# Squares of late chunks on ScalarE alone, statistics of token rows on GpSimd, and another order table

## The chip, the core and the metric

The kernel runs on one core of a Trainium2 chip. The metric is the time of the device for one execution, in microseconds (us); lower is better. The core has five engines that run side by side, each through its own list of instructions in the order of that list: TensorE (PE, matrix products into PSUM), VectorE (DVE), ScalarE (ACT), GpSimd (POOL) and SyncE (SP, which only issues DMAs). An instruction that waits holds up everything behind it on its engine.

## What is computed

Attention without softmax, normalised by token and head, and then a feed-forward layer on the 4608 tokens:

```python
kv = np.einsum('bhsd,bhse->bhde', k, v)          # 8 batches, 8 heads, 576 tokens, 64
out = np.einsum('bhsd,bhde->bhse', q, kv)
rms = np.sqrt(np.mean(out * out, axis=-1, keepdims=True) + 1e-06)
x = (out / rms * g_norm)                         # rows of 512 = 8 heads x 64
h = x @ w_in                                     # 512 -> 1024
solu = h * softmax(h)
ln = (solu - mu) / np.sqrt(var + 1e-06) * g_ln   # over the 1024
y = ln @ w_out                                   # 1024 -> 512
```

The softmax's denominator and the mean need not be applied to the elements. With e = exp(h) and u = h * e, the output rows are u @ (w_out scaled by g_ln and centred), times one factor for each token, and this factor follows from three sums over the 1024 features of a token: z = sum(e), usum = sum(u) and qsum = sum(u * u). "Statistics" below means the combination qsum - usum^2 / 1024 + 1e-6 * 1024 * z^2 (up to a common factor), whose reciprocal square root is the factor.

## The kernel before, in words

The 4608 tokens are nine chunks of 512. Chunks 0 to 7 hold the first 512 tokens (in the order of the load) of one batch each, chunk 8 the 64 that are left of every batch. The work is cut into some 700 named pieces. Each piece is a Python function that issues a few instructions; `plan.add` (in class `Plan`, line 34) gives it a name, the engine or engines on which it may run, the pieces that must stand ahead of it, and the buffers that it takes. The string `ORDER` (line 68) lists all pieces once, and the kernel issues them in that order. So the table fixes, for each engine, the order of its instructions, and with `@` and `/` also the buffer and the engine: `b3.1/act@ob6` is piece b3.1 on ScalarE into buffer ob6. Between engines nothing is ordered but by semaphores: a piece waits for what it reads and for the buffer that it takes over. A piece that stands early in the table on an idle engine runs early, whatever stands around it.

Buffers are slots (line 19): PSUM banks P0 to P2 (two banks each) and S0, S1; in SBUF L0 to L7 and M0 to M12 (large), osq, lss, rst, and ob0 to ob6 for output rows.

The pieces that the prediction speaks of, for chunk c, group m of 128 tokens, and half or part p:

- `k`, `v`, `q` (L269): load of a batch, 576 KB written as bf16 from f32, issued from GpSimd's queue (batches 0 and 1 in two halves `a`, `b` of 288 KB). `wi`, `wo` load the weights. The n-th DMA of that queue also waits until the one eight before it has landed.
- `kv` (L314) and its copies out of PSUM `kc` (L173 on ScalarE, L175 on VectorE): the 64x64 products of all heads of a batch.
- `qt`/`qc` (L359): q turned by TensorE for chunks 0 to 4. For chunks 5 to 8 `qx` (L370) turns it by a DMA transpose that SyncE issues.
- `o` (L407; L470 for chunks 6 to 8): out = q @ kv. For chunks 0 to 5 the squares `sq` (L420), their means by TensorE `s` (L435), `ln` (L439) and `ex` (L443) give the norm, and `x` (L453) applies it. For chunks 6 to 8 the tokens lie on the partitions: `sq` (L479), `vd` (L483), `vl` (L489, L491), `vg` on GpSimd (L495), `x` (L504), and `xt` (L512), a DMA transpose.
- `h`, the product with w_in: chunks 0 to 2 with features on the partitions (L572), chunks 3 to 8 with tokens (L581), two halves of four matmuls for each m, such as h4.00 and h4.01.
- `e` = exp(h) on ScalarE (L592; for token rows L599, which also sums z) and `u` on VectorE (L607; for token rows L612, with usum).
- `r`, the squares of u. For chunks 0 to 2 they are elements (L622 on ScalarE, L624 on GpSimd), summed later by TensorE with z and usum in `z` (L691), after `g` (L643) on GpSimd has added up e. For token rows `r` sums as it squares: L630 on ScalarE or L632 on VectorE, as the table says.
- `t` (L637): the rows of u turned by a DMA transpose from SyncE, chunks 3 to 8.
- `gate` (L343): a copy of one element on GpSimd that reads the last load, q of batch 7. The transposes t of all chunks from 3 on wait for it, and each qx waits for t3.0. So no DMA transpose is in flight beside the loads.
- `st`: the statistics (L703 to L708 for chunks 0 to 2; four small VectorE instructions, L714 to L720, for chunks 3 to 8), `rs` their reciprocal square root on ScalarE (L726, L728).
- `a` (L767; L774 for the last two quarters): product with w_out, two halves for each m. `b` (L782 on ScalarE, L784 on VectorE) multiplies by the factor into an ob buffer, and `d` (L799 for chunks 6 to 8, two DMAs each; L801) stores it, from the queue of SyncE, GpSimd or (chunk 8) ScalarE. `ql` copies the last rows of each q for chunk 8, `warm` are matmuls on zeros, `gb` loads g_norm for L495.

## Time and profile before

| | us |
|---|---|
| median of 3 runs | 182.08 (182.04 to 183.93) |
| the profiled execution, its own time | 181.77 |
| its span, first to last instruction | 179.7 |
| mean granted clock of TensorE | 0.999 of full speed |
| last matmul ends at | 174.86 |
| last load of q (batch 7): issued, landed | 70.94, 88.70 |

A page of the profile describes one execution. Times in it are from the start of the span. A group row gives the line, the engine, the operation, output and input, the count, then busy time and the mean ns of one, then the idle time of the engine just before these instructions and what ended it. A row of waits gives who waited for whom, and total, times, longest. A row of the DMA view gives the size of one DMA and the time from issue to landing. A timeline row gives start, length, engine, line and count; the engines' queues that only issue are written SPq, ACTq. In the chain of work that ended last, each piece is what released the next.

### The profile page before, as it was taken

The page shows a single profiled execution, that of the slowest core. Times are in us where ns is not written, and L with a number is a line of the kernel's source. Part 1 is how long each engine was busy: PE and PEld are TensorE (multiplying, and loading weights), DVE is VectorE, ACT ScalarE, POOL GpSimd, SP SyncE. Part 2 cuts the span into 40 slices and gives each one's busy share as a digit, 9 for nine tenths or more (in the row PEclk, how much of TensorE's full clock was granted, in tenths as well). Part 3 has the DMA queues.
Part 4 walks back from the last instruction along what each step waited for, and adds up shares of the span by engine and source line. Part 5 has one row for each costly group of instructions (what it writes and reads, how often), then busy time and mean ns, then how long its engine had stood idle before and what let it go on. Part 6 is the DMA issues. An engine that isn't in the chain of part 4 may idle for free.

```text
span 179.7 us, 4520 instructions
## 1 busy us (share of the span) xinstructions
PE 164.9 (92%) x1808; PEld 81.1 (45%) x1831; DVE 127.1 (71%) x222; ACT 128.1 (71%) x239; POOL 71.9 (40%) x83
## 2 busy tenths in 40 slices
...
DMA  5999999999999999999799999999998689968994
GB/s 170 252 207 275 353 208 209 205 208 222 248 233 232 209 207 198 277 214 206 157 172 203 206 216 220 152 256 245 171 227 239 99 166 248 200 139 215 175 256 125
DMA packets 60424, 37.81 MB, mean 210 GB/s; under 512 B 42140, under 2 KB 55204, under 8 KB 60404
## 3 DMA queue, kind: packets, MB, share of 16 engines
...
## 4 chain that ended last, share of the span: by engine, by line
PE 63%; DMA 22%; DVE 6%; issue 3%; POOL 1%; SPq 1%; ACT 1%; POOLq 0%; DVEq 0%; ACTq 0%
PE ps_S L767 20%; PE ps_P L581 19%; DMA sb_M<-in_q_dram 9%; PE ps_P L572 8%; PE ps_P L767 5%; DMA out_dram<-sb_ob 4%; DMA sb_L<-in_v_dram 4%; DMA sb_M<-sb_M 3%; PE ps_S L359 2%; DVE sb_ob L784 2%; PE ps_P L314 2%; PE ps_P L407 2%; DMA sb_L<-sb_L 2%; PE ps_P L691 1%; PE ps_S L435 1%
## 5 line engine op out<-in xcount | busy, mean ns | idle before, releaser
L767 PE MATMUL ps_S<-w_out_sb,sb_L 128*128 128x512 bf16 x220 | 53.1, 379 | 2.9 <-issue 2.4
L581 PE MATMUL ps_P<-w_in_sb,sb_M 128*128 128x512 bf16 x188 | 42.7, 379 | 1.0 <-ACT kvd L173 0.8
L767 PEld LDWEIGHTS <-sb_L 128*128 128x128 bf16 x280 | 26.4, 98 | 33.4 <-issue 3.3
L612 DVE SCALAR_TENSOR_TENSOR sb_L<-ps_P,sb_M 128x1024 bf16<-128x1024 f32 x24 | 29.1, 1222 | 8.4 <-ACT sb_M L599 8.2
L599 ACT ACTIVATE sb_M<-ps_P 128x1024 f32<-128x1024 f32 x24 | 24.5, 1023 | 8.2 <-PE ps_P L581 7.1
L581 PEld LDWEIGHTS <-sb_M 128*128 128x128 bf16 x192 | 18.7, 98 | 23.3 <-issue 0.9
L495 POOL TENSOR_TENSOR sb_M<-rr,g_rep 128x1024 f32<-128x1024 f32 x6 | 12.3, 2061 | 30.4 <-ACT rr L491 23.7
L572 PE MATMUL ps_P<-sb_M,w_in_sb 128*128 128x512 bf16 x94 | 21.9, 379 | 0.1
L607 DVE TENSOR_TENSOR sb_L<-ps_P,sb_M 128x1024 bf16<-128x1024 f32 x12 | 14.6, 1222 | 8.2 <-ACT sb_M L592 8.2
L453 DVE SCALAR_TENSOR_TENSOR sb_M<-ps_P,g_cols,sb_rst 128x512 bf16<-128x512 f32 x24 | 18.0, 790 | 2.9 <-ACT sb_rst L443 2.6
L784 DVE TENSOR_SCALAR sb_ob<-ps_S,rstd 128x512 f32<-128x512 f32 (+1 forms) x19 | 13.8, 735 | 7.7 <-PE ps_S L767 2.2
L592 ACT ACTIVATE sb_M<-ps_P 128x1024 f32<-128x1024 f32 x12 | 12.2, 1024 | 6.9 <-PE ps_P L572 6.9
L643 POOL TENSOR_TENSOR sb_M<-sb_M 128x512 bf16<-128x512 f32 x12 | 15.1, 1278 | 4.9 <-ACT sb_M L592 4.8
L420 ACT ACTIVATE sb_osq<-ps_P 128x512 bf16<-128x512 f32 x24 | 13.4, 596 | 4.6 <-PE ps_P L407 4.6
L630 ACT ACTIVATE sb_M<-sb_L 128x1024 bf16<-128x1024 bf16 x14 | 14.6, 1047 | 0.0
L572 PEld LDWEIGHTS <-w_in_sb 128*128 128x128 bf16 x96 | 9.2, 98 | 10.5 <-issue 0.2
L801 POOL DMA_DIRECT2D out_dram<-sb_ob x10 | 6.3, 633 | 16.4 <-DVE sb_ob L784 8.8
L632 DVE SCALAR_TENSOR_TENSOR sb_M<-sb_L 128x1024 bf16<-128x1024 bf16 x10 | 12.8, 1276 | 0.1
L443 ACT ACTIVATE sb_rst<-sb_lss 128x512 f32<-128x512 f32 x20 | 12.0, 632 | 0.1
L767 PE MATMUL ps_P<-w_out_sb,sb_L 128*128 128x512 bf16 x47 | 11.4, 379 | 0.1
L206 PE MATMUL ps_S<-zeros 128*128 128x512 bf16 (+1 forms) x18 | 8.5, 591 | 1.8 <-DVE zeros L188 1.5
L624 POOL TENSOR_TENSOR sb_L<-sb_L 128x1024 bf16<-128x1024 bf16 x4 | 7.6, 1910 | 6.1 <-DVE sb_L L607 6.0
...
## 6 DMA issues: line engine op xcount, KB each, us to landing
...
sb_L<-in_k_dram POOLq DMA_DIRECT2D x6, 576.0 KB, 12.2
sb_L<-in_v_dram POOLq DMA_DIRECT2D x6, 576.0 KB, 13.1
sb_M<-in_q_dram POOLq DMA_DIRECT2D x6, 576.0 KB, 12.3
...
sb_M<-in_q_dram POOLq DMA_DIRECT2D x4, 288.0 KB, 7.0
```

The lines of the kernel that those rows point to most:

```text
L420: nc.scalar.activation(out=t[:, :], in_=T["o", c, hf][:, z], func=AF.Square)
L453: nc.vector.scalar_tensor_tensor(out=T["x", c][:, pairs_of(c, hf), :, z], in0=T["o", c, hf][:, z].rearrange("p (n q) -> p n q", n=2), scal ...
L572: nc.tensor.matmul(t[:, f % 2], w_in_sb[:, dt, f * 128:(f + 1) * 128], T["x", c][:, dt].rearrange("p q z -> p (q z)"), start=(dt == 0), st ...
L581: nc.tensor.matmul(T["h", c, m][:, half], x_block(c, m, dt), w_in_sb[:, dt, half * 512:half * 512 + 512], start=(dt == 0), stop=(dt == NP ...
L599: nc.scalar.activation(out=t.rearrange("p a b -> p (a b)"), in_=T["h", c, m].rearrange("p a b -> p (a b)"), func=AF.Exp, accum_out=T["zsum ...
L607: nc.vector.tensor_tensor(out=flat(T["u", c][:, 2 * p:2 * p + 2, :]), in0=flat(T["h", c, p]), in1=flat(T["e", c, p]), op=MUL)
L612: nc.vector.scalar_tensor_tensor(out=T["un", c][:, m, :], in0=T["h", c, m].rearrange("p a b -> p (a b)"), scalar=1.0, in1=T["e", c, m].rea ...
L630: nc.scalar.activation(out=unused, in_=src, func=AF.Square, accum_out=by)
L632: nc.vector.scalar_tensor_tensor(out=unused, in0=src, scalar=1.0, in1=src, op0=MUL, op1=MUL, accum_out=by)
L643: nc.gpsimd.tensor_tensor(out=T["es", c][:, n, :], in0=e[:, 0, :], in1=e[:, 1, :], op=ADD)
L767: nc.tensor.matmul(T["acc", c, m][:, 0], T["u", c][:, f, m * 128:(m + 1) * 128], w_out_sb[:, f, :], start=(f == 0), stop=(f == NF - 1))
L784: nc.vector.tensor_scalar_mul(out=t[:, :], in0=src, scalar1=T["rstd", c][:, m:m + 1])
```

## The change

Three things change. First, the squares `r` of chunks 4 to 8 may only run on ScalarE; those of chunk 3 may still run on either, and all four are on VectorE in the new table. Second, the statistics of chunks 3 to 8 become six element-wise products and sums on GpSimd, with two constant tiles that VectorE fills once at the start. Third, the whole order table is another one. The change in the code:

```diff
@@ -197,6 +197,10 @@
     factors = big.tile([128, 4, 2], FP32, name="factors")
     nc.vector.memset(factors[:, :, 0:1], -1.0)
     nc.vector.memset(factors[:, :, 1:2], 1e-6 * d_ff * d_ff)
+    per_u = big.tile([128, 4], FP32, name="per_u")
+    nc.vector.memset(per_u, -1.0 / d_ff)
+    per_z = big.tile([128, 4], FP32, name="per_z")
+    nc.vector.memset(per_z, 1e-6 * d_ff)
 
 
     def warm(i):
@@ -675,7 +679,7 @@
                          [("M", ("e", c, m))], [("h", c, m)])
                 plan.add(f"u{c}.{m}", "dve", lambda c=c, m=m: row_u(c, m), [f"e{c}.{m}"] + [f"u{c}.0"] * (m > 0),
                          [] if m else [("L", ("un", c))], [("h", c, m), ("e", c, m)] + [("un", c)] * (m > 0))
-                plan.add(f"r{c}.{m}", ("act", "dve"), lambda e, c=c, m=m: row_usq(c, m, e), [f"u{c}.{m}"],
+                plan.add(f"r{c}.{m}", ("act", "dve") if c < 4 else ("act", "act"), lambda e, c=c, m=m: row_usq(c, m, e), [f"u{c}.{m}"],
                          uses=[("un", c), ("e", c, m)])
                 plan.add(f"t{c}.{m}", "sp", lambda c=c, m=m: u_turn(c, m), [f"u{c}.{m}"] + [f"t{c}.0"] * (m > 0) + ["gate"] * (c >= GATED),
                          [] if m or c == GATED else [("L", ("u", c))], [("un", c)] + [("u", c)] * (m > 0 or c == GATED))
@@ -707,19 +711,19 @@
         T["vare", c] = small.tile([128, 4], FP32, name="vare")
         nc.vector.tensor_reduce(out=T["vare", c][:, :], in_=terms[:, :, :], op=ADD, axis=mybir.AxisListType.X)
 
-    def row_stats(c, ms=slice(0, 4)):
-        zs, us, qs = (T[name, c][:, ms] for name in ("zsum", "usum", "qsum"))
-        n = ms.stop - ms.start
-        a = small.tile([128, n], FP32, name="a")
-        nc.vector.scalar_tensor_tensor(out=a[:, :], in0=us, scalar=-1.0 / d_ff, in1=us, op0=MUL, op1=MUL)
-        d = small.tile([128, n], FP32, name="d")
-        nc.vector.scalar_tensor_tensor(out=d[:, :], in0=zs, scalar=1e-6 * d_ff, in1=zs, op0=MUL, op1=MUL)
-        f = small.tile([128, n], FP32, name="f")
-        nc.vector.tensor_tensor(out=f[:, :], in0=a[:, :], in1=qs, op=ADD)
-        T["vare", c] = small.tile([128, n], FP32, name="vare")
-        nc.vector.scalar_tensor_tensor(
-            out=T["vare", c][:, :], in0=f[:, :], scalar=1.0, in1=d[:, :], op0=MUL, op1=ADD
-        )
+    def row_stats(c):
+
+        def product(name, in0, in1, op):
+            t = small.tile([128, 4], FP32, name=name)
+            nc.gpsimd.tensor_tensor(out=t[:, :], in0=in0[:, :], in1=in1[:, :], op=op)
+            return t
+
+        a = product("a", T["usum", c], T["usum", c], MUL)
+        a = product("a2", a, per_u, MUL)
+        f = product("f", a, T["qsum", c], ADD)
+        d = product("d", T["zsum", c], T["zsum", c], MUL)
+        d = product("d2", d, per_z, MUL)
+        T["vare", c] = product("vare", f, d, ADD)
 
     def rstd(c):
         lv = small.tile([128, 4], FP32, name="lv")
@@ -735,7 +739,7 @@
             plan.add(f"y{c}", "dve", lambda c=c: sums_turn(c), [f"z{c}"], uses=[("sum", c)])
             plan.add(f"st{c}", "dve", lambda c=c: stats(c), [f"y{c}"], uses=[("sum", c)])
         else:
-            plan.add(f"st{c}", "dve", lambda c=c: row_stats(c), [f"{n}{c}.{m}" for n in "eur" for m in range(4)])
+            plan.add(f"st{c}", "pool", lambda c=c: row_stats(c), [f"{n}{c}.{m}" for n in "eur" for m in range(4)])
         plan.add(f"rs{c}", "act", lambda c=c: rstd(c), [f"st{c}"])
```

The table, where the prediction follows it (in the new kernel all line numbers of the functions are higher by 4):

```diff
 ORDER = """
-warm0@S0 k0a@L0,L1 v0a rsqrt q0a@M0 k0b ident qt0.0@S0 cast0.0/act cast0.1/dve kv0a@P0 kc0a.1/act v0b q0b wi0
-kc0a.2/act gr warm1@S1 tg@S1 qc0.0/dve@M1 kc0a.0/act o0.0@P0 sq0.00@osq0 sq0.01@osq1 warm2@S0 kv0b@P1 kc0b.0/act
-kc0b.1/dve s0.00@S0 ex0.00@rst0 kc0b.2/act qt0.1@P2 qc0.1/dve s0.01@S0 ex0.01@rst1 warm3@P1 o0.1@P2 sq0.10@osq1
-sq0.11@osq0 warm4@S0 s0.10@S0 warm5@P1 gm@M2 x0.00@M1 ex0.10@rst0 s0.11@S1 x0.01 x0.10 ex0.11@rst1 x0.11 wi1
-h0.0+@P0 wo0@L2 h0.1+ h0.2+@P1 h0.3+ h0.0 h0.1 h0.2 wo1@L3 table e0.0@M3 u0.0@L1 h0.4+@P2 k1a@L0 h0.5+ v1a h0.3 h0.4
-e0.1@M4 h0.5 e0.2@M5 h0.6+@P0 h0.7+ q1a@M6 k1b v1b g0.0@M7 g0.1 g0.2 r0.0/act@L4 h0.6 h0.7 e0.3@M1 g0.3 wm0@S1 u0.1
-r0.1/act u0.2 u0.3 r0.2/act r0.3/act wm1 wc4 kv1a@P2 kc1a.1/act kc1a.0/act warm6@S0 qt1.0@S0 z0@P0 warm7@P1
-kc1a.2/act wc1 wc2 qc1.0/act@M1 o1.0@P2 warm8@S0 wc3 sq1.00@osq0 sq1.01@osq1 kv1b@P1 kc1b.1/act kc1b.2/act wc5 wc0
...
-s2.10@S1 s2.11@P1 ln2.10@lss1 g1.0@M8 g1.1 g1.2 b0.3/dve@ob0 ln2.11@lss0 a1.00@S0 ex2.10@rst2 ex2.11@rst3 x2.00@M3
-q4@M0 k5@L1 v5 x2.01 x2.10 r1.1/pool r1.2/pool r1.3/act ql3/act a1.01 kv3@P2 kc3.1/act qt3.0@S1 x2.11 h2.0@P0 h2.1
-h2.2@P1 h2.3 kc3.0/act qc3.0/act@M4 d0.2/sp d0.3/sp kc3.2/act h2.4@P2 h2.5 g1.3 q5@M5 qt3.1@S1 e2.0@M9 g2.0@M7
-e2.1@M10 e2.2@M11 u2.0@L4 u2.1 h2.6@P0 h2.7 e2.3@M3 g2.1 g2.2 qc3.1/dve u2.2 k6@L2 qt4.0@S1 o3.0@P1 sq3.00@osq0
-qc4.0/dve@M10 r2.0/act@L6 r2.1/pool u2.3 r2.2/act z1@P2 y1 st1 rs1 b1.0/dve@ob0 d1.0/sp a1.10@S1 a1.11 a1.20@P0
-r2.3/act s3.00@P2 ln3.00@lss0 a1.21 b1.1/dve@ob2 b1.2/dve@ob1 g2.3 z2@S0 sq3.01@osq0 y2 ex3.00@rst3 st2 o3.1@P2
-sq3.10@osq1 s3.01@S1 ln3.01@lss0 a1.30@P0 sq3.11@osq0 ex3.01@rst2 s3.10@S0 ln3.10@lss1 ex3.10@rst0 x3.00@M4 x3.01
-a1.31 a2.00@S1 s3.11@S0 ln3.11@lss0 kv4@P1 ex3.11@rst2 kc4.0/act a2.01 v6 q6@M3 k7@L0 rs2 b1.3/dve@ob3 v7 q7@M7
-d1.1/sp d1.2/sp x3.10 kv5@P0 kc4.2/dve kc5.1/act kc4.1/dve o4.0@P1 sq4.00@osq0 x3.11 ql5/pool qt4.1@S0 qc4.1/act
-sq4.01@osq1 kc5.0/dve kc5.2/dve h3.00@P2 h3.01 h3.10@P0 e3.0@M8 b2.0/dve@ob1 s4.00@S0 ln4.00@lss0 s4.01@S1
-ln4.01@lss1 h3.11 e3.1@M11 ex4.00@rst2 a2.10@S0 a2.11 u3.0@L1 u3.1 ex4.01@rst0 x4.00@M1 x4.01 o4.1@P2 a2.20@S1
-b2.1/act@ob2 a2.21 d1.3/pool gate@L3 t3.0 t3.1 qx5@M10 sq4.10@osq1 s4.10@S0 sq4.11@osq0 s4.11@P0 b2.2/dve@ob0
-ln4.10@lss1 ln4.11@lss0 r3.0/dve ex4.10@rst0 ex4.11@rst2 x4.10 h3.20@P1 h3.21 h3.30@P0 qx6@M8 x4.11 h3.31 h4.00@P2
-h4.01 e3.2@M9 u3.2 e3.3@M4 e4.0@M12 r3.1/act r3.2/dve a2.30@S0 u3.3 t3.2 t3.3 d2.0/sp h4.10@P1 u4.0@L5 h4.11
-r3.3/dve e4.1@M11 u4.1 gb r4.0/act h4.20@P0 h4.21 h4.30@P2 st3 e4.2@M4 u4.2 h4.31 e4.3@M1 o5.0@P1 sq5.00@osq0
-sq5.01@osq1 rs3 a2.31 a3.00@S1 s5.00@P0 ln5.00@lss0 b2.3/dve@ob3 u4.3 a3.01 b3.0/dve@ob4 ex5.00@rst2 x5.00@M12
-s5.01@S0 ln5.01@lss1 kv6@P0 kc6.1/dve kc6.2/dve t4.0@L4 d2.1/sp t4.1 t4.2 kc6.0/dve o5.1@P2 sq5.10@osq1 ex5.01@rst0
-sq5.11@osq0 d2.2/pool x5.01 a3.10@S1 s5.10@S0 ln5.10@lss1 ql7/pool a3.11 b3.1/act@ob0 o6.0@P0 o6.1@P1 sq6.0@rst0
-ql1/dve s5.11@S0 ln5.11@lss0 d2.3/sp a3.20@S1 a3.21 a3.30@S0 ex5.10@rst2 ex5.11@rst3 t4.3 vd6.0 vl6.0 vg6.0@M8
-b3.2/dve@ob2 x5.10 x5.11 sq6.1@rst0 vd6.1 x6.0@M6 qx7@M10 ql6/dve r4.1/act a3.31 r4.2/act a4.00@S1 a4.01 r4.3/dve
-h5.00@P2 h5.01 vl6.1 b3.3/act@ob3 xt6.0@M8 kv7@P0 kc7.0/dve kc7.1/act a4.10@S0 a4.11 st4 kc7.2/act h5.10@P0 vg6.1@M4
-x6.1 xt6.1 e5.0@M1 ql2/act u5.0@L5 r5.0/dve h5.11 h5.20@P1 h5.21 t5.0@L0 ql4/dve qx8@M0 e5.1@M4 u5.1 e5.2@M1 u5.2
-rs4 b4.0/act@ob1 b4.1/act@ob5 r5.1/dve h5.30@P2 h5.31 e5.3@M12 u5.3 d3.0/sp d3.1/pool d3.2/pool h6.00@P0 h6.01
...
-b6.0/dve@ob3 b6.1/dve@ob1 d5.3/pool u8.0@L4 st7 rs7 a6.20@P1 a6.21 b6.2/act@ob4 a6.30@S0 a6.31 a7.00@S1 d6.0/pool
-h8.20@P0 h8.21 u8.1 h8.30@P2 r8.0/act r8.1/act b6.3/dve@ob3 t7.2 t7.3 t8.0@L1 e8.2@M1 h8.31 e8.3@M12 a7.01 a7.10@S0
-u8.2 a7.11 a7.20@P1 a7.21 a7.30@P0 t8.1 d6.1/sp d6.2/pool d6.3/sp b7.0/act@ob5 d7.0/pool b7.1/act@ob0 r8.2/dve
-b7.2/act@ob2 a7.31 d7.1/sp a8.00@S0 a8.01 a8.10@S1 a8.11 t8.2 u8.3 r8.3/dve t8.3 a8.20@P2 a8.21 b7.3/dve@ob4 d7.2/sp
-d7.3/sp st8 rs8 b8.0/dve@ob5 d8.0/act a8.3|0@S0 a8.3|1@P0 b8.1/dve@ob0 d8.1/act b8.2/act@ob3 b8.3|0/dve@ob1 d8.2/act
-b8.3|1/dve@ob2 d8.3|0/act d8.3|1/sp
+k0a@L0,L1 v0a warm0@S0 q0a@M0 ident qt0.0@S0 rsqrt cast0.0/act cast0.1/act kv0a@P0 kc0a.1/dve kc0a.0/act k0b v0b q0b
+gr tg@S1 warm1@P1 kc0a.2/dve qc0.0/dve@M1 o0.0@P1 warm2@S0 kv0b@P0 wi0 wi1 sq0.00@osq0 s0.00@S0 ex0.00@rst0 wo0@L2
+wo1@L3 qt0.1@P2 warm3@S0 qc0.1/dve k1a@L4 sq0.01@osq0 v1a q1a@M2 gm@M3 x0.00@M4 k1b kc0b.0/act v1b kc0b.2/act
+kc0b.1/act o0.1@P0 sq0.10@osq1 s0.01@S0 warm4@S1 s0.10@S1 warm5@P2 ex0.01@rst1 x0.01 sq0.11@osq0 s0.11@S0 h0.0+@P1
+h0.1+ h0.2+@P2 h0.3+ ex0.10@rst0 x0.10 ex0.11@rst1 q1b k2@L1 x0.11 h0.0 h0.1 h0.2 table e0.0@M1 u0.0@L0 ql0/act
+g0.0@M5 h0.3 e0.1@M6 u0.1 g0.1 h0.4+@P0 h0.5+ h0.4 h0.5 e0.2@M0 u0.2 wm0@S0 h0.6+@P1 wm1 wc3 r0.0/act@L5 wc6 wc2 v2
+q2@M6 h0.6 h0.7+ h0.7 e0.3@M4 kv1a@P0 kc1a.2/dve warm6@S1 qt1.0@S1 warm7@P2 kc1a.0/act kc1a.1/act qc1.0/act@M3 wc5
+r0.1/pool r0.2/act o1.0@P2 sq1.00@osq0 sq1.01@osq1 warm8@S1 wc1 kv1b@P0 kc1b.2/act u0.3 s1.00@S1 g0.2 g0.3 wc4
+qt1.1@P1 ln1.00@lss0 s1.01@S1 wc7 kc1b.0/act k3@L6 r0.3/pool wc0 a0.00@S0 qc1.1/dve kc1b.1/act o1.1@P1 v3 q3@M4
+ln1.01@lss1 ex1.00@rst1 ex1.01@rst0 z0@S1 x1.00@M3 x1.01 k4@L2 v4 sq1.10@osq1 sq1.11@osq0 s1.10@P2 s1.11@P0
...
+ex2.01@rst0 h1.7+ h1.6 h1.7 e1.3@M3 a0.20@S1 o2.1@P2 sq2.10@osq1 g1.2 g1.3 x2.00@M5 x2.01 u1.3 a0.21 a0.30@S0 a0.31
+s2.10@P1 sq2.11@osq0 s2.11@P0 b0.2/act@ob2 r1.2/act r1.3/pool a1.00@S1 a1.01 ln2.10@lss1 ln2.11@lss0 ex2.10@rst0
+x2.10 k5@L0 ex2.11@rst1 x2.11 z1@P0 y1 st1 rs1 ql2/dve qt3.0@P1 b0.3/dve@ob3 b1.0/dve@ob4 v5 h2.0@P2 q5@M3
+qc3.0/dve@M6 k6@L3 v6 q6@M1 h2.1 ql4/act e2.0@M8 k7@L5 u2.0@L4 v7 h2.2@P0 h2.3 h2.4@P1 e2.1@M7 u2.1 qt3.1@S1
+qc3.1/act kv3@P2 kc3.1/act kc3.0/act g2.0@M9 h2.5 h2.6@P0 kc3.2/dve h2.7 o3.0@P2 q7@M10 a1.10@S1 e2.2@M8
+r2.0/pool@L7 r2.1/act ql1/dve e2.3@M5 sq3.00@osq0 a1.11 sq3.01@osq1 a1.20@S0 u2.2 u2.3 s3.00@P1 g2.1 s3.01@P0 g2.2
+g2.3 r2.2/act ln3.00@lss0 ln3.01@lss1 r2.3/pool a1.21 a1.30@P1 ex3.00@rst1 b1.1/dve@ob5 ex3.01@rst0 b1.2/dve@ob6
+x3.00@M5 d0.0/sp o3.1@P0 d0.1/sp d0.2/sp d0.3/sp x3.01 sq3.10@osq1 sq3.11@osq0 z2@S1 s3.10@S0 ln3.10@lss1 s3.11@P2
+ln3.11@lss0 d1.0/sp ql5/pool a1.31 a2.00@S0 ex3.10@rst0 ex3.11@rst1 a2.01 b1.3/act@ob4 y2 st2 rs2 x3.10 qt4.0@S1
+qt4.1@P1 x3.11 h3.00@P0 kv4@P2 kc4.1/dve b2.0/dve@ob3 kc4.2/dve gate@L2 qc4.0/act@M9 qc4.1/act h3.01 h3.10@P1 h3.11
+kc4.0/dve e3.0@M0 u3.0@L1 t3.0 qx5@M6 e3.1@M8 o4.0@P2 sq4.00@osq0 sq4.01@osq1 ql3/dve u3.1 a2.10@S0 a2.11
+b2.1/dve@ob2 r3.0/dve s4.00@S1 ln4.00@lss0 kv5@P0 gb kc5.1/dve kc5.2/act o4.1@P1 sq4.10@osq0 sq4.11@osq2 s4.01@S1
+ln4.01@lss1 a2.20@S0 a2.21 kc5.0/dve ex4.00@rst1 ex4.01@rst0 x4.00@M0 s4.10@S1 ln4.10@lss0 x4.01 r3.1/dve
+b2.2/act@ob1 ex4.10@rst1 x4.10 h3.20@P0 ql7/pool h3.21 e3.2@M9 d1.1/sp u3.2 s4.11@S1 ln4.11@lss0 ex4.11@rst1 x4.11
+h3.30@P2 h3.31 e3.3@M5 u3.3 r3.2/dve r3.3/dve a2.30@S0 a2.31 t3.1 o5.0@P0 h4.00@P1 t3.2 h4.01 b2.3/act@ob0
+sq5.00@osq2 sq5.01@osq0 e4.0@M3 s5.00@S0 h4.10@P2 u4.0@L4 ln5.00@lss0 t3.3 t4.0@L1 s5.01@S1 ln5.01@lss1 ex5.00@rst1
+x5.00@M5 ex5.01@rst0 x5.01 qx6@M9 h4.11 e4.1@M8 u4.1 t4.1 a3.00@S0 a3.01 a3.10@S1 o5.1@P0 st3 kv6@P1 kc6.0/dve
+d1.2/sp rs3 b3.0/act@ob5 kc6.1/dve a3.11 d1.3/pool d2.0/sp qx7@M6 sq5.10@osq0 s5.10@S0 sq5.11@osq2 kc6.2/act d2.1/sp
+s5.11@P2 ln5.10@lss1 ln5.11@lss0 ex5.10@rst0 ex5.11@rst1 h4.20@P1 h4.21 r4.0/act e4.2@M4 h4.30@P2 h4.31 e4.3@M0
+x5.10 x5.11 h5.00@P0 h5.01 u4.2 u4.3 t4.2 d2.2/pool d2.3/pool d3.0/sp b3.1/act@ob6 e5.0@M3 a3.20@S0 u5.0@L3 a3.21
+a3.30@S1 b3.2/dve@ob3 kv7@P2 kc7.0/dve r4.1/act kc7.2/dve r4.2/act t4.3 o6.0@P1 sq6.0@rst1 kc7.1/act h5.10@P0 h5.11
+e5.1@M10 vd6.0 a3.31 b3.3/dve@ob2 a4.00@S0 a4.01 a4.10@S1 t5.0@L2 u5.1 t5.1 vl6.0 vg6.0@M4 x6.0@M8 r4.3/act st4
+r5.0/act o6.1@P0 h5.20@P2 h5.21 h5.30@P1 h5.31 sq6.1@rst1 vd6.1 xt6.0@M4 rs4 d3.1/pool b4.0/dve@ob5 e5.2@M9 u5.2
+a4.11 a4.20@S0 b4.1/dve@ob0 a4.21 h6.00@P2 vl6.1 e5.3@M5 u5.3 vg6.1@M3 x6.1 xt6.1 r5.1/act r5.2/act o7.0@P1
+sq7.0@rst1 d3.2/sp h6.01 e6.0@M3 h6.10@P0 h6.11 ql6/pool qx8@M9 t5.2 t5.3 a4.30@S1 r5.3/act e6.1@M1 vd7.0 vl7.0
+vg7.0@M8 u6.0@L4 r6.0/act u6.1 t6.0@L5 t6.1 r6.1/act a4.31 h6.20@P2 b4.2/dve@ob3 b4.3/dve@ob6 x7.0@M3 xt7.0@M8 h6.21
...
+x8.0@M9 vl8.1 vg8.1@M1 t6.2 x8.1 xt8.0@M6 xt8.1 a6.00@S1 a6.01 a6.10@S0 a6.11 r6.2/act r6.3/act st6 h7.00@P2 h7.01
+e7.0@M3 u7.0@L2 h7.10@P1 h7.11 e7.1@M1 u7.1 h7.20@P0 h7.21 h7.30@P2 e7.2@M4 u7.2 h7.31 h8.00@P1 d5.2/pool r7.0/act
+rs6 b6.0/act@ob2 h8.01 e7.3@M3 e8.0@M8 u7.3 u8.0@L3 h8.10@P0 h8.11 t6.3 e8.1@M9 r7.1/act r7.2/act a6.20@S1
+b6.1/dve@ob5 t7.0@L1 a6.21 d5.3/pool r7.3/act h8.20@P2 h8.21 h8.30@P1 h8.31 a6.30@S0 b6.2/act@ob3 u8.1 a6.31
+b6.3/dve@ob1 e8.2@M3 e8.3@M6 u8.2 u8.3 a7.00@S1 a7.01 t7.1 a7.10@S0 a7.11 t7.2 a7.20@P2 t7.3 a7.21 a7.30@P1
+d6.0/pool t8.0@L4 r8.0/act r8.1/act r8.2/act a7.31 d6.1/sp d6.2/sp t8.1 t8.2 t8.3 st7 rs7 b7.0/dve@ob3 r8.3/act
+b7.1/dve@ob5 b7.2/dve@ob2 b7.3/dve@ob6 a8.00@S0 a8.01 a8.10@S1 a8.11 a8.20@P1 a8.21 d6.3/pool d7.0/sp d7.1/sp
+d7.2/sp st8 rs8 b8.0/act@ob1 b8.1/act@ob5 a8.3|0@S1 d7.3/sp b8.2/dve@ob2 d8.0/sp d8.1/act d8.2/act b8.3|0/dve@ob6
+d8.3|0/sp a8.3|1@S0 b8.3|1/dve@ob1 d8.3|1/sp
 """
```

22 lines of the change are left out of this document (7 added, 15 removed).

## The prediction

> **What bounds the kernel now.** I read the page's first two parts, the waits of TensorE with its busy time in two stretches, the chain that ended last, and then the timelines of GpSimd and SyncE around the one DMA inside that chain.
>
> ```profile
> span 179.7 us, 4520 instructions
> ...
> PE 164.9 (92%) x1808; PEld 81.1 (45%) x1831; DVE 127.1 (71%) x222; ACT 128.1 (71%) x239; POOL 71.9 (40%) x83
> ...
> DMA  5999999999999999999799999999998689968994
> ```
> ```profile
> PE ps_S L767 <- issue: 2.4, 5, 1.7
> ...
> PE ps_P L581 <- ACT kvd L173: 0.8, 1, 0.8
> PE ps_P L407 <- DMA sb_M<-sb_M: 0.4, 1, 0.4
> ```
> ```profile
> 97.81:174.86 77.05, 75.40 (x678) 36.28 (x688) 61.35 (x106) 55.30 (x115) 19.86 (x19) 1.00 1.00 201
> 27.57:97.81 70.24, 66.89 (x925) 34.08 (x935) 50.79 (x89) 54.85 (x99) 34.00 (x36) 1.00 1.14 213
> ```
>
> TensorE is the bound: 92% of the span, and in the last 77.05 us of its work (the columns are length, TensorE, weight loads, VectorE, ScalarE, GpSimd) it is idle for 1.65. It does the same set of matmuls before and after, so the new order can only remove waits or make new ones: 3.35 us are left to remove in the earlier stretch, 1.65 in the later one. VectorE and ScalarE end few of these waits, so work taken off VectorE is worth next to nothing by itself.
>
> One thing the order cannot move is the gate. The loads of q, k and v go out on GpSimd's queue; `gate` (L343) waits for the last of them, q7; only then does SyncE issue transposes, and q5's (qx5, L370) must land before o5.0 (L407), which starts at 97.81:
>
> ```profile
> 92.04 5.72 DMA sb_M<-sb_M
> ```
> ```profile
> 25.18 0.72 POOL L269 DMA_DIRECT2D sb_M<-in_q_dram  x1
> ...
> 37.22 0.62 POOL L801 DMA_DIRECT2D out_dram<-sb_ob  x1 [5.99 <-DVE sb_ob L784]
> ...
> 52.48 0.75 POOL L269 DMA_DIRECT2D sb_L<-in_k_dram  x1
> ...
> 70.94 0.75 POOL L269 DMA_DIRECT2D sb_M<-in_q_dram  x1 [0.47 <-PE ps_S L691]
> ```
> ```profile
> 88.83 0.18 POOL L343 COPY sb_L<-sb_M 1x1 bf16<-1x1 bf16 x1 [13.32 <-DMA sb_M<-in_q_dram]
> ```
> ```profile
> 41.22 29.34 SPq L801 DMA_DIRECT2D out_dram<-sb_ob  x6
> 89.04 2.84 SPq L637 DMA_TRANSPOSE sb_L<-sb_L  x2
> 92.04 6.95 SPq L370 DMA_TRANSPOSE sb_M<-sb_M  x2
> ```
>
> qx5, issued at 92.04, lands 5.7 later, at 97.77; TensorE had been ready 0.4 us (the wait above), since 97.4. The forecast hangs on these two times in the new order.
>
> **The change part by part.** *When TensorE is ready for o5.0.* Of the pieces ahead of o5.0, the eight halves h4.00 to h4.31 now stand behind it, and a2.31 has come ahead: 32 matmuls less, 4 more, net 28.
>
> ```profile
> 92.09 5.34 PE L581 MATMUL ps_P<-w_in_sb,sb_M 128*128 128x512 bf16 x24
> ```
>
> 24 of them take 5.34 us, the last one 0.38, so they start every 0.216 us and 28 are 6.0 us. With the waits of before, TensorE is ready at 97.4 - 6.0 = 91.4.
>
> *When the gate opens.* The DMA engines are full until 88 us (the page's DMA row), so the loads end when their bytes are through, not when GpSimd issues them.
>
> ```profile
> 32.00:40.00 8.00, 6.27 (x41) 3.05 (x42) 3.11 (x5) 5.62 (x15) 2.12 (x3) 1.00 1.21 207
> ```
> ```profile
> sb_M<-in_q_dram POOLq DMA_DIRECT2D x1, 288.0 KB, 6.7
> ```
> ```profile
> sb_M<-in_q_dram POOLq DMA_DIRECT2D x1, 576.0 KB, 17.8
> ```
>
> q1b, issued at 25.18, landed 6.7 later, at 31.9; q7, issued at 70.94, landed 17.8 later, at 88.7. Between them lie the 18 loads of chunks 2 to 7, each 0.59 MB written at 207 GB/s (last column), 2.84 us: 51.1 in all. The other 5.7 us are the seven stores issued in between (d0.0 on GpSimd's queue, six on SyncE's), 0.8 each. After the change five are left: d0.0 to d0.3 and d1.0, while d1.1 and d1.2 stand behind t3.0, which waits for the gate. So the gate opens 1.6 us earlier; 0 if stores were free, 2.5 if they took as long per byte as the loads (0.26 MB). The engines do not run dry either: k5 follows a1.00 in both tables and went out at 52.48, and the loads ahead of it last until 31.9 + 9 x 2.84 + 3 x 0.8 = 59.9.
>
> *From gate to qx5.* Before, t3.0 and t3.1 go out first, 2.84 us for two; now t3.0 alone: 1.4 us earlier.
>
> ```profile
> sb_M<-sb_M SPq DMA_TRANSPOSE x9, 5.2
> ```
>
> The landing itself took 5.7, the median of the nine is 5.2; with one transpose less in front I take 0.3 off, between 0 and 0.5. qx5 lands at 97.77 - 1.6 - 1.4 - 0.3 = 94.45; bounds 93.3 and 96.4.
>
> TensorE, ready at 91.4, then waits 3.05 us where it waited 0.4. Any other wait ahead of o5.0, new or gone, vanishes in this one: those of the head, and that of z2, whose r2.0 and r2.3 are now on GpSimd behind q7's issue. Term: +2.7 us, and the work behind o5.0 cannot give it back, as TensorE is full there.
>
> *Squares (r).* Of 24, ten run on VectorE before, four (chunk 3) after. ScalarE gains six.
>
> ```profile
> L630 ACT ACTIVATE sb_M<-sb_L 128x1024 bf16<-128x1024 bf16 x14 | 14.6, 1047 | 0.0
> ...
> L632 DVE SCALAR_TENSOR_TENSOR sb_M<-sb_L 128x1024 bf16<-128x1024 bf16 x10 | 12.8, 1276 | 0.1
> ```
>
> 6.3 us onto ScalarE, 7.7 off VectorE. The stretch where it matters is o5.0 to a4.31, 35.5 us of TensorE in the new table, where ScalarE has ten e, ten r, four each of sq, ln and ex, three b, three sq of rows, and small pieces.
>
> ```profile
> L599 ACT ACTIVATE sb_M<-ps_P 128x1024 f32<-128x1024 f32 x24 | 24.5, 1023 | 8.2 <-PE ps_P L581 7.1
> ...
> L443 ACT ACTIVATE sb_rst<-sb_lss 128x512 f32<-128x512 f32 x20 | 12.0, 632 | 0.1
> ```
>
> 10 x 1.02 + 10 x 1.05 + 12 x 0.6 + 3 x 0.7 + 3 x 1.02, and an estimated 2.8 for the rest: 35.9 us, as much as TensorE has. Before, ScalarE's share from 97.81 on is 55.30 of 77.05. It has no slack left, and in its queue b3.1 waits for ob6, which d1.2 frees only after t3.3, t4.0, qx6 and t4.1 on SyncE; behind b3.1 stand e5.0 and sq6.0, for which h5.10 and x6.0 wait. I take +0.5 us: 0 would be ScalarE keeping up because it starts this stretch with an empty queue, 2 that it stalls for about a store's landing.
>
> *Statistics.* Four VectorE instructions for each of six chunks become six on GpSimd.
>
> ```profile
> L643 POOL TENSOR_TENSOR sb_M<-sb_M 128x512 bf16<-128x512 f32 x12 | 15.1, 1278 | 4.9 <-ACT sb_M L592 4.8
> ...
> L714 DVE SCALAR_TENSOR_TENSOR a<-usum 128x4 f32<-128x4 f32 x6 | 1.1, 189 | 0.0
> ...
> masks.py:199 POOL TENSOR_SCALAR_AFFINE_SELECT eye<-eye 9x9 f32<-9x9 f32 x1 | 0.2, 192 | 0.1
> ```
>
> On GpSimd the nearest by size is the 9x9 row, 0.19 us: 1.15 a chunk, against 0.75 for four like L714; the far end is 128x512, 7.7 a chunk. The cover is the matmuls between the last r of a chunk and the first bank that its b must free. It is thinnest at the end: b8.0 can start when a8.01 is done, 12 halves (10.4 us) after h8.31, and r8.3 is done there after e8.3, four r and rs7, some 5.7; 4.7 us are left for st8 and rs8. I take 0; at the far end it would cost 3.5.
>
> *What goes.* The wait of 0.8 (L581 on a kvd copy) goes: kv7's bank now serves h5.20, seven halves later. -0.75.
>
> *The end.* d8.3|0 moves from ScalarE's queue to SyncE's, just ahead of the last store, d8.3|1.
>
> ```profile
> 174.32 2.46 ACTq L799 DMA_DIRECT2D out_dram<-sb_ob  x4
> ```
>
> Each issue takes 0.6 us; of the two new ones ahead of the last store about half lies beside the last scale: +0.3, between 0 and 0.6 (half of 1.2).
>
> **Sum**: 2.7 + 0.5 - 0.75 + 0.3 = +2.75 on the profiled execution's 181.77 (its span of 179.7 and 2.07 around it): 184.5. That execution lies 0.3 below the median of the runs, 182.08, so I forecast 184.8.
>
> **The rivals.** *Hidden gate.* If qx5 lands by 91.4, o5.0 does not wait: -0.4 + 0.5 - 0.75 + 0.3 gives 181.7, and 180.0 if the "issue" wait of 1.7 goes as well. The price is the 2.7 of the sum; it decides from a gate that opens at 85.6, 1.5 us earlier than my 87.1. Loads alone would end at 31.9 + 51.1 = 83.0, so the stores would have to be nearly free or the transposes quicker than any bound above. Against it stand the full DMA row and the 207 GB/s. The Trainium skill's page "DMA: Bandwidth & Descriptors", section "Anatomy of one DMA — SWDGE (gpsimd) path", speaks for it: it prices the bytes at 436 KB per us, by which a load would be an estimated 1.35 us, the loads over by about 60 us, and the time 181.7. The trace disagrees, with 2.84 us a load.
>
> *ScalarE becomes the bound.* With 35.9 against 35.5 us it falls behind at b3.1 and again on the chain sq6.1, vl6.1, vg6.1, x6.1, xt6.1 to h6.20: 2 us more than forecast, 187. For it speaks the missing slack; against it that it starts the stretch with an empty queue.
>
> *The change does nothing that counts*: VectorE gets 10 us lighter and TensorE does not notice. That is already in my forecast; alone, with the order as it was, it would be 182.
>
> **How the numbers follow.** Forecast 0.60 (183 to 186.5, by the bounds of qx5's landing), 0.10 of it under 183.9; ScalarE 0.14; hidden gate 0.26, 0.06 of it under 180.3. One per cent, 1.8 us, is about what a measurement of this kernel can tell from no change. Faster 0.06; same 0.20 + 0.10 = 0.30; slower 0.50 + 0.14 = 0.64. The range, 182.2 to 187.2, leaves out most of the hidden gate and the far end of ScalarE.
>
> **What would show it.** After the change: TensorE's wait at o5.0 (L411) on the DMA into sb_M about 3 us; the gate's copy (L347) near 87.2 and qx5 issued some 1.8 us later; no wait of TensorE above 0.5 us behind o5.0 but around h5.10, h6.00 and h6.20; VectorE's busy time some 10 us lower, ScalarE's some 4 higher, since copies and scales move the other way. I am wrong if the gate's copy runs before 85.6, if o5.0 does not wait, or if idle time of TensorE of over 2 us appears elsewhere behind o5.0.

## The result and the profile after

The changed kernel takes 192.3 us (median of four executions, 190.8 to 194.1) against 182.3 before: a ratio of 1.050, 95% interval 1.039 to 1.062. I had forecast 184.8, with 187.2 as the end of the range. The direction was right, the size was missed by a factor of more than three. The mean granted clock of these executions was 0.985 or 0.975, the longer times at the lower clock, and the ratios here leave out the executions that were lengthened most.

The profiled execution took 190.84 us, 9.1 more than the profiled one of before. Its page, first lines:

```profile
span 188.9 us, 4525 instructions
...
PE 168.3 (89%) x1809; PEld 81.5 (43%) x1831; DVE 120.4 (64%) x189; ACT 131.0 (69%) x247; POOL 83.4 (44%) x119
...
PEclk9999999999999999999999999999999789999997
```

VectorE's busy time fell by 6.7 us and ScalarE's rose by 2.9, but TensorE is idle more often, and two slices of the clock's row ahead of the last stand below 9 (a 7 and an 8, at 146 to 156 us). The two longest groups of TensorE's waits (us in total, times, longest):

```profile
PE ps_S L771 <- ACT sb_ob L786: 2.9, 2, 2.7
PE ps_P L439 <- DVE sb_L L611: 2.6, 2, 1.9
```

Neither stood among its waits before. The wait that I had forecast, o5.0 (L411) on a DMA into sb_M, is not in TensorE's list. It shows as a short wait of the weight load. The timeline from the gate to o5.0:

```profile
87.01 1.22 DVE L636 SCALAR_TENSOR_TENSOR sb_M<-sb_L 128x1024 bf16<-128x1024 bf16 x1
87.05 1.22 POOL L347 COPY sb_L<-sb_M 1x1 bf16<-1x1 bf16 x1 [12.75 <-DMA sb_M<-in_q_dram]
...
88.30 1.32 SPq L641 DMA_TRANSPOSE sb_L<-sb_L  x1
...
89.80 3.57 SPq L374 DMA_TRANSPOSE sb_M<-sb_M  x1
...
96.54 0.14 PEld L411 LDWEIGHTS <-kvd 64*64 64x64 bf16 x8 [0.52 <-DMA sb_M<-sb_M]
```

The gate's copy starts at 87.05, where I had 87.1. Then it takes 1.22 us where it took 0.18: VectorE's square r3.0 runs beside it for just that time. qx5 goes out at 89.80, and o5.0 starts at 96.54, when qx5 has landed. TensorE had come only half a microsecond earlier: it was 4.6 us later than the 91.4 I had worked out. Two late paths ended together, and so the DMA's share is almost hidden. qx5 took 6.7 us from issue to landing, where I had 5.4.

Of TensorE's own delay ahead of o5.0, 2.6 us come from one VectorE instruction, in the timeline from 57 to 80 us:

```profile
64.06 1.91 POOL L628 TENSOR_TENSOR sb_L<-sb_L 128x1024 bf16<-128x1024 bf16 x1
...
64.57 5.15 DVE L175 COPY q_last<-sb_M 128x256 bf16<-128x256 bf16 x1
...
65.92 3.70 POOL L647 TENSOR_TENSOR sb_M<-sb_M 128x512 bf16<-128x512 f32 x3
...
69.64 2.34 DVE L611 TENSOR_TENSOR sb_L<-ps_P,sb_M 128x1024 bf16<-128x1024 f32 x2
```

The copy is ql1. It moves 256 elements a row and takes 0.2 us elsewhere; here it ends at 69.72, when GpSimd's four instructions (r2.0, g2.1, g2.2, g2.3) have ended at 69.62. u2.2 and u2.3 (L611) follow 5 us late, and TensorE waits for the banks that they free. Another 1.36 us is a wait at 90.7, also new: kc5.1 stands behind r3.0 on VectorE, and kc5.2, sq4.10 and the ln that frees TensorE's bank stand behind kc5.1 on ScalarE.

Behind o5.0, the stretch to the last matmul, with length and TensorE's busy time, then the stop inside it:

```profile
96.54:184.21 87.67, 83.69 (x707) 39.71 (x716) 56.51 (x81) 64.95 (x134) 28.01 (x56) 0.98 0.96 189
```
```profile
134.51 7.59 SPq L641 DMA_TRANSPOSE sb_L<-sb_L  x4
142.22 2.15 SPq L516 DMA_TRANSPOSE sb_M<-sb_M  x1
144.42 2.53 SPq L805 DMA_DIRECT2D out_dram<-sb_ob  x4
```
```profile
out_dram<-sb_ob SPq DMA_DIRECT2D x1, 256.0 KB, 2.6
```
```profile
147.07 0.69 ACT L786 ACTIVATE sb_ob<-ps_S,rstd 128x512 f32<-128x512 f32 x1 [3.34 <-issue]
...
147.81 5.30 PE L771 MATMUL ps_S<-w_out_sb,sb_L 128*128 128x512 bf16 x16 [2.66 <-ACT sb_ob L786]
```

87.67 us, against 77.05 before plus the 6.0 of the 28 matmuls that now stand behind: 4.6 more. ScalarE's scale b5.2 starts at 147.07. The profile calls its wait "issue", since it shows no event for it, but the order table tells what it needs: slot ob2, last used by b3.3, whose store d3.3 is the first of the four stores that SyncE issues at 144.42. That store lands 2.6 us later, at 147.0. It stood behind qx8, t5.2, t5.3, t6.0, t6.1 and xt7.0 in SyncE's queue. TensorE needs the bank that b5.2 frees and stops for 2.66 us. After the stop its 16 matmuls take 5.30 us. The windows view shows why (length, TensorE's busy time, granted clock):

```profile
148.80:152.40 3.60, 3.60 (x11) 0.53 0.76 144
```

The clock was halved for about 3.4 us; 11 matmuls where 16 or 17 fit.

So the 9.2 us of the span are: 4.7 at o5.0 (96.54, where before's 97.81 less 6.0 is 91.81), 4.6 behind it (2.7 of stop, 1.7 of half clock, 0.2 of the rest), and -0.1 at the tail.

### The profile page after: what moved, and what is told of

Its sections match the earlier page's. It is cut to its first block, busy times and chain, and to the rows that moved or that the text cites. A ratio compares the mean times of both kernels' runs of the same rounds, so it can differ in the third digit from the quotient of the medians.

```text
span 188.9 us, 4525 instructions
## 1 busy us (share of the span) xinstructions
PE 168.3 (89%) x1809; PEld 81.5 (43%) x1831; DVE 120.4 (64%) x189; ACT 131.0 (69%) x247; POOL 83.4 (44%) x119
## 3 DMA queue, kind: packets, MB, share of 16 engines
q10 hardware_dynamic: 592, 1.11, 1.8%
## 4 chain that ended last, share of the span: by engine, by line
PE 55%; DMA 18%; DVE 8%; POOL 7%; issue 5%; ACT 4%; SPq 1%; DVEq 0%; POOLq 0%
PE ps_P L585 21%; PE ps_S L771 19%; DMA sb_M<-in_q_dram 16%; PE ps_P L771 4%; DVE q_last L175 3%; DMA out_dram<-sb_ob 2%; POOL sb_M L647 2%; POOL sb_L L628 2%; DVE sb_L L611 2%; PE ps_P L576 2%; POOL sb_L L273 2%; PE ps_S L439 2%; PE ps_P L318 2%; PE ps_P L474 1%; PE ps_P L411 1%
## 5 line engine op out<-in xcount | busy, mean ns | idle before, releaser
L771 PE MATMUL ps_S<-w_out_sb,sb_L 128*128 128x512 bf16 x242 | 58.8, 388 | 3.4 <-ACT sb_ob L786 2.9
L585 PE MATMUL ps_P<-w_in_sb,sb_M 128*128 128x512 bf16 x185 | 43.2, 379 | 0.8 <-issue 0.3
L771 PEld LDWEIGHTS <-sb_L 128*128 128x128 bf16 x280 | 27.3, 99 | 36.7 <-issue 6.5
L499 POOL TENSOR_TENSOR sb_M<-rr,g_rep 128x1024 f32<-128x1024 f32 x6 | 11.3, 1897 | 31.9 <-ACT rr L495 31.9
L634 ACT ACTIVATE sb_M<-sb_L 128x1024 bf16<-128x1024 bf16 x20 | 20.9, 1047 | 0.0
L788 DVE TENSOR_SCALAR sb_ob<-ps_S,rstd 128x512 f32<-128x512 f32 (+1 forms) x21 | 14.9, 721 | 7.4 <-PE ps_S L771 5.7
L611 DVE TENSOR_TENSOR sb_L<-ps_P,sb_M 128x1024 bf16<-128x1024 f32 x12 | 14.5, 1219 | 4.2 <-ACT sb_M L596 4.2
L628 POOL TENSOR_TENSOR sb_L<-sb_L 128x1024 bf16<-128x1024 bf16 x7 | 13.3, 1899 | 3.0 <-DVE sb_L L611 3.0
L786 ACT ACTIVATE sb_ob<-ps_S,rstd 128x512 f32<-128x512 f32 x12 | 8.2, 687 | 8.7 <-PE ps_S L771 3.7
L175 DVE CAST kvd<-ps_P 64x256 bf16<-64x256 f32 (+2 forms) x15 | 5.9, 394 | 10.8 <-PE ps_P L318 9.3
L508 DVE TENSOR_TENSOR sb_M<-ps_P,sb_M 128x1024 bf16<-128x1024 f32 x6 | 7.3, 1221 | 4.7 <-POOL sb_M L499 4.6
```

The source lines that it names most:

```text
L585: nc.tensor.matmul(T["h", c, m][:, half], x_block(c, m, dt), w_in_sb[:, dt, half * 512:half * 512 + 512], start=(dt == 0), stop=(dt == NP ...
L611: nc.vector.tensor_tensor(out=flat(T["u", c][:, 2 * p:2 * p + 2, :]), in0=flat(T["h", c, p]), in1=flat(T["e", c, p]), op=MUL)
L628: nc.gpsimd.tensor_tensor(out=dst, in0=src, in1=src, op=MUL)
L634: nc.scalar.activation(out=unused, in_=src, func=AF.Square, accum_out=by)
L771: nc.tensor.matmul(T["acc", c, m][:, 0], T["u", c][:, f, m * 128:(m + 1) * 128], w_out_sb[:, f, :], start=(f == 0), stop=(f == NF - 1))
L788: nc.vector.tensor_scalar_mul(out=t[:, :], in0=src, scalar1=T["rstd", c][:, m:m + 1])
```

## The experiments

My theory after seeing the result: o5.0 is held by the gate, much as forecast; the slow copy and the blocked gate come from VectorE and GpSimd sharing something; the store behind the transposes makes the stop, and the stop makes the half clock. The rivals: the copy is a loss of its own; ScalarE has no slack, and the store is an accident; the moved work costs wherever it stands.

**e1_copy: the slow copy elsewhere.**

```diff
-... z1@P0 y1 st1 rs1 ql2/dve qt3.0@P1 ...
+... z1@P0 y1 st1 rs1 ql2/dve ql1/dve qt3.0@P1 ...
-... r2.0/pool@L7 r2.1/act ql1/dve e2.3@M5 ...
+... r2.0/pool@L7 r2.1/act e2.3@M5 ...
```

> The changed kernel with one piece moved: ql1, the VectorE copy that took 5.15 us beside GpSimd, goes right behind ql2, where GpSimd only issues DMAs. Both theories expect the copy at 0.22 us and the 2.65 us of TensorE's waits at 69 to 72 gone. Theory (the gate is the floor for o5.0): o5.0 still starts at qx5's landing, near 96.5, TensorE waits about 2.7 us there on the DMA, and the time is the same within 0.5 us (190.5 to 191.3 for a profiled execution of 190.8). Rival (the slow copy is a loss of its own): o5.0 starts near 94 and the time falls by 2.3 to 2.9.

Measured: 187.16 us in the profiled execution, ratio 1.029 (1.021 to 1.037). Two executions took 187.2 and 187.8 us at a granted clock of 1.000, two 191.5 and 191.8 at 0.982: the clock is a large part of this ratio. The result is neither "the same" nor the rival's o5.0 near 94. Three rows:

```profile
PE ps_S L771 <- ACT sb_ob L786: 2.6, 1, 2.6
...
PE ps_P L411 <- DMA sb_M<-sb_M: 1.5, 1, 1.5
```
```profile
145.87 3.61 PE L771 MATMUL ps_S<-w_out_sb,sb_L 128*128 128x512 bf16 x16 [2.59 <-ACT sb_ob L786]
```

TensorE's two waits at 69 to 72 are gone, and a wait of 1.5 us on the DMA has taken their place at o5.0, which starts at 95.47: the gate is a floor. Its copy no longer ran beside a square (0.18 us), and qx5 went out at 89.18. The start of o5.0 accounts for 1.1 of the 3.6 us of span that went. Another 1.69 is the clock: the same stop of 2.6 us, but the 16 matmuls behind it took 3.61 us, not 5.30. No half clock followed in this execution, so a stop of this length does not always bring it, and one stretch of it costs 1.69 us. The last 0.8 lies between o5.0 and the stop, where the changed kernel's trace has five waits of 0.16 to 0.21 us and this one none; what they are stays open.

**e2_store: the store d3.3 ahead of the transposes.**

```diff
-... sq7.0@rst1 d3.2/sp h6.01 ...
+... sq7.0@rst1 d3.2/sp d3.3/sp h6.01 ...
-... st5 u6.3 d3.3/sp a5.00@S1 ...
+... st5 u6.3 a5.00@S1 ...
```

> The changed kernel with one piece moved: the store d3.3 goes right behind d3.2 on SyncE's queue, ahead of qx8 and seven transposes. Theory (b5.2 waits for slot ob2, whose store was stuck in that queue, and the half clock follows from the stop): the 2.66 us wait of TensorE at 145 goes, and with it the 3.4 us at half clock, 1.7 of cost; 4.0 to 4.6 us less, 186.2 to 186.8. Rival (ScalarE has no slack, and b5.2 would be late without this store): less than 1 us gained. Second rival (the half clock is no consequence of the stop): 2.5 to 2.8 us gained, the half clock still there.

Measured: median 189.2 us, ratio 1.038 (1.031 to 1.046), some 3 us less than the changed kernel.

```profile
PE ps_S L771 <- ACT sb_ob L786: 1.1, 2, 0.8
```
```profile
72.80:76.60 3.80, 3.80 (x59) 0.55 1.22 208
```

The stop fell from 2.66 to 0.76 us and no half clock followed it. The stretch from o5.0 to the last matmul took 84.2 us instead of 87.7: 3.5 less. What is left, 0.76, is b5.2 behind other work in ScalarE's queue, so the rival holds for that part. In this execution the clock was halved elsewhere, at 73 us, right behind the two waits that the slow copy makes. These two things do not explain all of the miss against 4.0 to 4.6: two executions at a clock of 1.000 and 0.998 took 188.7 and 189.7. The rest stays open.

**e3_three: copy, store and the gate's neighbour together.** The edits of e1 and e2, and r3.0 behind kc5.0, so that no two-input VectorE instruction runs beside the gate:

```diff
-... b2.1/dve@ob2 r3.0/dve s4.00@S1 ...
+... b2.1/dve@ob2 s4.00@S1 ...
-... kc5.0/dve ex4.00@rst1 ...
+... kc5.0/dve r3.0/dve ex4.00@rst1 ...
```

> The changed kernel with ql1 behind ql2, d3.3 behind d3.2, and r3.0 (a VectorE square with two SBUF inputs, beside which the gate's copy on GpSimd took 1.22 us where it took 0.18 before) behind kc5.0. Theory: the gate's copy takes 0.2 us, qx5 goes out 1.0 us earlier and o5.0 starts near 95.5; with the 4.3 us of the store the time falls by 5.0 to 5.6, to 185.2 to 185.8. Rival (the gate's copy was not held up by the square): no more than e2 gives, and if the slow copy is a loss of its own, 6.5 to 7.

Measured: median 185.6 us (184.1 to 186.7), ratio 1.016 (1.008 to 1.024), 6.7 below the changed kernel.

```profile
PE ps_P L411 <- DMA sb_M<-sb_M: 2.7, 1, 2.7
```
```profile
87.84 1.33 SPq L641 DMA_TRANSPOSE sb_L<-sb_L  x1
89.34 3.90 SPq L374 DMA_TRANSPOSE sb_M<-sb_M  x1
```

This comes close to the kernel that I had forecast: o5.0 waits 2.7 us for qx5 (forecast 3.05), qx5 goes out at 89.34 (89.04), and the median is 185.6 (184.8). The two disturbances had stood on top of it. Moving r3.0 did a second thing: the 1.36 us of TensorE's wait at 90.7 fell to 0.27. The agreement is not exact. The profiled execution is the longest of the four, 186.67, 4.9 above before's: o5.0 starts 3.6 behind 91.81, since qx5 took 6.0 us to land; the stretch behind it takes 83.45 us, 0.4 above the 83.05 of before, where the sum had it 0.25 below; and 0.8 more pass after the last matmul. The one wait of TensorE left behind o5.0 is 1.03 us on a transpose, ahead of a6.00; none on ScalarE is listed there. The expectations of e5, e7 and e9 count from 184.1, the shortest of e3's four executions.

**e4_stats: the statistics back on VectorE**, their six GpSimd products replaced by the four instructions of before.

> The changed kernel with the statistics of chunks 3 to 8 back on VectorE, four instructions a chunk, at their places in the table. Theory (they are off the path): same within 0.5 us, 190.3 to 191.3. Rival (six instructions of GpSimd per chunk delay rs and b): 1 to 3 us faster.

Measured: median 193.2, ratio 1.059 (1.052 to 1.067), against 1.050 (1.039 to 1.062) for the changed kernel: no gain. In the new table the products cost nothing that shows. The trace shows one thing more. Here the square started after the gate's copy, which took 0.18 us, and qx5 went out at 88.48, 1.3 earlier; but the slow copy was there (5.51 us), and o5.0 started at 96.53 all the same, with no wait on the DMA. So TensorE's own delay was enough by itself to hold o5.0 there.

**e5_squares: e3 with the squares on the engines of before** (r4.3, r5.0, r5.1, r6.1, r7.2, r8.2, r8.3 on VectorE).

> e3_three with the squares of chunks 4 to 8 on the engines that the kernel before gave them (six more on VectorE: r4.3, r5.0, r5.1, r6.1, r7.2, r8.2, and r8.3), at their places in the new table. Theory (part one costs what b5.2 waits behind ScalarE's queue): TensorE's wait of 1.03 us ahead of a6.00 falls below 0.4, and the time by 0.5 to 1.0 from 184.1. Rival (ScalarE has room): the wait stays and the time is the same within 0.3. Second rival (VectorE becomes late): 0.5 to 2 us slower.

Measured: ratio 1.033 (1.027 to 1.039), some 3 us slower than e3. The second rival holds:

```profile
PE ps_S L771 <- DVE sb_ob L788: 1.9, 2, 1.1
```

Now it is VectorE's scales that come late. The new table counts on ScalarE for these squares; table and placement cannot be judged apart.

**e6_parts: both moves of work in the old table**, with every r of chunks 4 to 8 written "/act" and no other edit of the order.

> The kernel before with its own order table, and only the two changes of work: squares of chunks 4 to 8 on ScalarE, statistics of token rows as six products of GpSimd. Theory (the new table costs, not the work moved): 181.5 to 182.8 against 182.1. Rival (the moved work costs wherever it stands): 184 or more.

Measured: 185.3 us, ratio 1.018 (1.013 to 1.023): the rival. I had taken the moves for harmless by themselves. Next, which of them.

**e10_stats_old: the statistics alone in the old table.**

> The kernel before with its own table, and only the statistics of token rows as six products of GpSimd. Theory (of the two moves of work, the squares cost the 3 us of e6_parts: r8.2 stands on ScalarE ahead of what frees a bank): the same as before within 0.5 us. Rival (the products, which share a port with VectorE, cost as much): 183.5 or more.

Measured: median 184.3, ratio 1.012 (1.004 to 1.019). The theory fell again: the products, free in the new table, cost some 2 us in the old one. GpSimd's and VectorE's timelines:

```profile
158.31 0.20 POOL L718 TENSOR_TENSOR f<-a,qsum 128x4 f32<-128x4 f32 x1 [3.24 <-issue]
...
159.52 2.14 POOL L803 DMA_DIRECT2D out_dram<-sb_ob  x4 [0.30 <-issue]
```
```profile
164.16 0.75 DVE L788 TENSOR_SCALAR sb_ob<-ps_S,rstd 128x512 f32<-128x512 f32 x1 [5.81 <-DMA out_dram<-sb_ob]
```

The third product of st7 waits on GpSimd for r7.3 until 158.3. Behind it in GpSimd's queue stands the store d6.0, which went out at 155.2 before. b6.3 needs its slot and waits 5.8 us; TensorE stops for 1.7.

**e12_queue: the same with d6.0 ahead of st7.**

```diff
-... b6.1/dve@ob1 d5.3/pool u8.0@L4 st7 ...
+... b6.1/dve@ob1 d5.3/pool d6.0/pool u8.0@L4 st7 ...
-... a7.00@S1 d6.0/pool h8.20@P0 ...
+... a7.00@S1 h8.20@P0 ...
```

> e10_stats_old (the kernel before, its table, statistics as six products of GpSimd) with one piece moved: the store d6.0, also on GpSimd's queue, goes ahead of st7. In e10_stats_old st7's products waited on GpSimd for r7.3 until 158.3, d6.0 went out behind them, b6.3 waited for its slot and TensorE stopped 1.7 us at 163. Theory (the products cost nothing themselves, but what is queued behind them does): TensorE's stop at 163 falls below 0.3 us and the time to 182.0 to 182.8, from 183.9 to 184.5. Rival (the products cost by sharing a port with VectorE): 183.5 or more.

Measured: 183.4 us, ratio 1.008 (1.004 to 1.011). The stop at 163 is gone, so the queue was its cause, but only about 0.8 us of the 2 came back. Where the other 1.2 arise stays open; the waits of TensorE behind o5.0 that are longer than before's are small (0.97 us at 117, where before has 0.75, and 0.48 at 138).

**e7_fill: e3 with h4.00 to h4.11 ahead of o5.0**, to cover the gate.

```diff
-... t3.1 o5.0@P0 h4.00@P1 t3.2 h4.01 ...
+... t3.1 h4.00@P1 h4.01 e4.0@M3 h4.10@P2 u4.0@L4 h4.11 o5.0@P0 t3.2 ...
```

> e3_three with the halves h4.00 to h4.11 (16 matmuls, 3.5 us, with e4.0 and u4.0) ahead of o5.0 instead of behind it. Theory (o5.0 waits 2.69 us for qx5, and TensorE has nothing ready in front of it): the wait falls below 0.3 and the time by 2.2 to 2.7, to 181.4 to 181.9 from 184.1. Rival (the time is given back behind o5.0, because ScalarE cannot follow): less than 1 us gained.

Measured: median 184.8, ratio 1.013 (1.010 to 1.016). The wait at o5.0 was gone, but less than 1 us gained, as the rival had it, though for another reason.

```profile
95.52 1.02 ACT L603 ACTIVATE sb_M<-ps_P 128x1024 f32<-128x1024 f32 x1 [3.08 <-DMA sb_M<-sb_M]
```
```profile
97.75 0.86 PE L439 MATMUL ps_S<-sb_osq,head_mean 128*128 128x512 bf16 x2 [1.20 <-ACT sb_osq L424]
```

e4.0 writes slot M3, and the table has q5 in M3, which qx5 still reads: ScalarE waits 3.1 us for the very DMA that was to be covered, sq5.00 stands behind e4.0, and TensorE waits at s5.00 instead. Where the new table has these halves, behind o5.0, the slot is free.

**e8_reduce: the copy as another instruction.** In the changed kernel, VectorE's copies of the last tokens become a sum over one element, at their old places:

```diff
-        copy(engine, q_last[:, :, b, :], T["q", b][:, :, 8, :])
+        with nc.allow_low_precision(reason="one term"): (nc.vector.tensor_reduce(out=q_last[:, :, b, :], in_=T["q", b][:, :, 8, :].rearrange("p n (d o) -> p n d o", o=1), op=ADD, axis=mybir.AxisListType.X) if engine == "dve" else copy(engine, q_last[:, :, b, :], T["q", b][:, :, 8, :]))
```

> The changed kernel with its table, and the copies of the last tokens on VectorE written as a sum over one element (a reduction), an instruction of the same data on the same engine at the same place. Theory (the plain copy needs a port of SBUF that GpSimd holds, a reduction does not): 0.3 to 0.6 us in place of 5.15, TensorE's 2.65 us of waits at 69 to 72 gone; the time as e1_copy had it, 187.0 to 188.9. Rival (VectorE waits for something that the records do not name, whatever the instruction): it takes some 5 us again, and the time stays at 190.8 or more.

Measured: ratio 1.029 (1.025 to 1.033), the same as e1, and again 187.4 and 187.9 us at a granted clock of 1.00 beside 190.3 and 191.0 at 0.976. The instruction at the old place of the slow copy, with GpSimd's beside it:

```profile
65.67 0.42 DVE L356 TENSOR_REDUCE q_last<-sb_M 128x256 bf16<-128x256 bf16 x1
```
```profile
65.25 1.91 POOL L628 TENSOR_TENSOR sb_L<-sb_L 128x1024 bf16<-128x1024 bf16 x1
67.11 3.71 POOL L647 TENSOR_TENSOR sb_M<-sb_M 128x512 bf16<-128x512 f32 x3
```

0.42 us beside the first of the same four GpSimd instructions, and TensorE's waits at 69 to 72 are gone. It was the kind of instruction beside GpSimd, not a missing input.

**e9_qx5: e3 with qx5 ahead of t3.0** on SyncE's queue (and a second element copied by the gate, into qx5's target tile, so that it still waits).

> e3_three with qx5 ahead of t3.0 on SyncE's queue; so that it still waits for the gate, the gate copies a second element, into qx5's target tile. Theory (o5.0 starts when qx5 lands, and that is one transpose too late): qx5 goes out 1.4 us earlier, o5.0 starts near 94.0 in place of 95.4, its wait falls from 2.7 to about 1.3, and the time by 1.2 to 1.6, to 182.5 to 182.9 from 184.1. Rival (the landing is set by the traffic, not by the issue): o5.0 within 0.4 of 95.4 and the time the same.

Measured: ratio 1.012 (1.007 to 1.018), median 184.6.

```profile
PE ps_P L411 <- DMA sb_M<-sb_M: 0.6, 1, 0.6
```
```profile
87.24 2.87 SPq L374 DMA_TRANSPOSE sb_M<-sb_M  x1
```

qx5 went out 2.1 us earlier, 0.6 of it because the gate opened earlier in this execution, and landed 0.6 sooner after its issue; o5.0 started 2.7 us earlier, at 92.64. So its landing follows its issue. The wait fell from 2.7 to 0.6; 1.0 us of the gain arrived in the median.

**e11_both: e9 with d3.2 and d3.3 on GpSimd's queue.**

> e9_qx5 with d3.2 and d3.3 on GpSimd's queue in place of SyncE's, so that qx8 and t5.2 to t6.1 go out up to 1.2 us earlier. Theory (a6.00 waits 1.0 us for t6.0, which stands behind them): that wait falls below 0.4 and the time by 0.6 to 1.0 from e9_qx5, to 181.6 to 182.2, level with the kernel before. Rival (b5.2 behind ScalarE's queue is what comes last there): within 0.3 us of e9_qx5.

Measured: median 184.4, ratio 1.009 (1.005 to 1.013). TensorE's wait ahead of a6.00 is gone from the trace, but the time is within 0.3 of e9's, as the rival had it. (The profiled execution took 185.7: TensorE stopped there for 2.5 us at 61, and half clock followed.) It is the best version of the new table that I found, and still about 0.9% behind the kernel before.

## Why the prediction was wrong

*What held.* TensorE stayed the bound. The gate opened at 87.05 (forecast 87.1), so the count of loads and stores was right; that it agrees to 0.05 us is luck, since the gate's copy started between 86.76 and 88.17 in the other kernels with this table. The kvd wait went. The six products took 0.20 us each but for two of over 1 us beside a square (0.19 forecast) and cost nothing in the new table (e4). The mechanism of the sum, o5.0 waiting about 3 us for qx5 because h4 had gone behind it, was there (e3: 2.7), and the kernel without the disturbances takes 185.6, 0.8 from the forecast. Some luck is in that 0.8, since the single terms of e3's profiled execution were further off (e3).

*First failing step: "Any other wait ahead of o5.0, new or gone, vanishes in this one."* That is so as long as these waits stay below the 3.05 us of the gate. They came to 4.6, and the landing of qx5 moved from 94.45 to about 96.5, past my bound of 96.4: 0.8 at the issue, 1.3 in the landing. So the term of +2.7 measured 4.7. TensorE's delay alone was enough for that: with the gate's copy undisturbed, o5.0 stayed at 96.53 (e4). With the slow copy gone as well it came at 95.47, on the DMA (e1). The landing of qx5 was mis-sized on its own account. I had taken 0.3 off 5.7 us for one transpose less in front, but wherever o5.0 waited for qx5 behind t3.0 it took 6.0 to 6.7 us (the changed kernel, e1, e3, e5, e8); why stays open. The slow copy and the slow gate I had not priced, because I had taken an instruction's duration as its own, whatever runs beside it. The trace of before showed otherwise, in two rows that I had not looked up, a copy of the same size and GpSimd beside it:

```profile
111.91 1.51 DVE L175 COPY q_last<-sb_M 128x256 bf16<-128x256 bf16 x1
```
```profile
111.43 1.90 POOL L495 TENSOR_TENSOR sb_M<-rr,g_rep 128x1024 f32<-128x1024 f32 x1 [1.61 <-ACT rr L491]
```

1.51 us beside GpSimd, 0.22 without. The new order set such a copy beside four GpSimd instructions in a row, which the order table shows. The Trainium skill states the mechanism in "SBUF — State Buffer", section "Who interferes with whom": VectorE and GpSimd share one pair of ports under an exclusive lock, a copy may need it, a reduction never does, and an instruction with two inputs in SBUF contends with GpSimd's reads. e8 and the gate's copy beside r3.0 agree. The page has the first to issue hold the pair for its whole instruction; here the copy stood through the running instruction and three more that came after it.

*Second: the +0.5 for ScalarE.* I had the mechanism, a scale waiting for a slot whose store stands behind transposes in SyncE's queue, and its far end (2, "about a store's landing"). But I looked for it at b3.1 alone and took it for a matter of ScalarE's load. It struck at b5.2, and cost 2.66 us; e2 took away 1.9 of it with one store. ScalarE's load itself cost about what I had said: the 0.76 left in e2.

*Third: no term for the clock.* Before, it stayed full until after the last matmul, so a stop was priced at its length. After the stop of 2.66 us the clock was halved for 3.4 us, 1.7 more. In each trace the clock changes only at whole steps of 3.41 us, counted from one fixed start, so TensorE's idle time can be counted in windows from step to step (length, TensorE's busy time, granted clock). The changed kernel:

```profile
145.53:148.94 3.41, 1.13 (x6) 1.00 1.05 347
148.94:152.36 3.42, 3.42 (x10) 0.50 0.76 144
```

The same for e1:

```profile
141.35:144.76 3.41, 1.93 (x9) 1.00 0.88 218
144.76:148.18 3.42, 2.31 (x11) 1.00 1.05 296
```

The stop of the changed kernel left one such window idle for 2.28 us, and half clock followed. In e1 the border of two windows cut the 2.59 us into 1.48 and 1.11, in e3 the 2.69 us at o5.0 into 1.09 and 1.60, and none followed. From 10 us to the last matmul of the fourteen traces (both kernels and the twelve runs), half clock followed every window that was idle for 1.94 us or more (five), none of 1.60 or less that ran at full clock, and two of the four between (1.63 to 1.72). The Trainium skill has this in "TensorE: Matmul & The Clock Gate", section "What's actually happening": the activity is judged over free-running windows of 3413 ns, and after an idle one the clock is at half. The length agrees. The page asks for one idle window of about 3.4 us, while here 1.63 to 2.51 us idle within one were enough. That the cost depends on where the stop falls in the window agrees with the page's free-running window; no run here moved a stop on purpose.

*And a gap in "what of it lies beside other work":* I priced the statistics by what waits for rs and b, not by what stands behind them on GpSimd's queue. In the new table that did no harm; in the old one the same code costs 1.2% (e10).

*A reading that was wrong without harm.* For the hidden gate I had priced a load at 1.35 us by the bytes that it writes, 0.59 MB, at the 436 KB per us that the Trainium skill states in "DMA: Bandwidth & Descriptors", section "Anatomy of one DMA — SWDGE (gpsimd) path". A load reads twice as many bytes, 1.18 MB of f32; by these the same figure gives an estimate of 2.7 us, close to the 2.84 us of the trace. The page does not say which bytes count, so it was no evidence for that rival.
